# Moving two key copies a batch to ScalarE, constant products in TensorE's waits, and the last output tile in two halves

## The chip, the cores and the metric

The kernel runs on one core of one Trainium2 chip. The core has five engines with a queue of instructions each: TensorE (PE; its weight loads are listed as PEld), VectorE (DVE), ScalarE (ACT), GpSimd (POOL) and SyncE (SP); 16 DMA engines move data. TensorE reads its operands from SBUF and writes to PSUM, which VectorE and ScalarE read. The metric is the time of the program on the device in microseconds (us); smaller is better. The profile is one execution, taken by the hardware profiler.

## What is computed

Two layers follow each other: chunked attention with a few memory keys, and a mixture of experts with noisy top-2 routing over its output.

```python
# attention: q, k, v are (4 batches, 8 heads, 768, 64); mem_k, mem_v (4, 8, 8, 64)
for c in range(nc):                       # 24 chunks of 32 queries
    l_start, r_end = max(0, c_start - 16), min(S, c_end + 8)
    k_full = np.concatenate([mem_k, k[:, :, l_start:r_end]], axis=2)
    v_full = np.concatenate([mem_v, v[:, :, l_start:r_end]], axis=2)
    scores = scale * np.matmul(q_c, k_full.transpose(0, 1, 3, 2))
    a = softmax(scores)
    out[:, :, c_start:c_end] = np.matmul(a, v_full)
# experts: x is (3072, 512), 8 experts, w1 (8, 512, 1024), w2 (8, 1024, 512)
noisy_logits = x @ w_gate + np.log1p(np.exp(x @ w_noise)) * noise
top2 = the two largest of each token; top2_w = softmax over the two
for e in range(8):
    for k in range(2):
        mask = top2[:, k] == e
        out[mask] += top2_w[mask, k, None] * (np.maximum(x[mask] @ w1[e], 0) @ w2[e])
```

## The kernel before

**Attention.** The four batches have three steps each, 12 in all (`NT`; step `i` is batch `i // 3`, position `tp = i % 3`); a step handles two tiles of 128 queries for all eight heads, taken as four pairs. TensorE, ScalarE, VectorE and SyncE follow an order written out by hand in the loop from L568; each engine works through its queue in that order.

A step runs: `scores(i + 1)` for the next step (L408; first eight small products with the memory keys, then, for tile j = 0 and 1 and each of the four pairs, four products with the keys; VectorE then takes the maximum `mx` and subtracts it into `sc`); `turn_p` (L439: TensorE transposes the probabilities, ScalarE copies them to `pT`); `turn_x` for the step before (L472: the same for the step's output `x`, copied to `xT` by ScalarE); `values` (L448: sums and products with the values into `ps_o`, which VectorE divides into the rows of x at L466); `exps` (L434, ScalarE); `gate` for the step before (L481: the router's logits).

**The turn of a batch.** Queries and keys arrive in natural order and have to be turned: `turn` (L393) takes one unit, a pair's queries or keys, through 12 transposes on TensorE into one of three PSUM banks used in rotation. `turns` (L552) copies the result to `qT` or `kT`. A unit of queries is one copy; a unit of keys is two copies of 64 partitions. `KS` (L562) says which engine copies each of the four key units: 1 is ScalarE, 0 VectorE; before, units 0 and 2 are ScalarE's and 1 and 3 VectorE's, so each has four copies a batch. `PLAN` puts the keys at the end of the batch's middle step, so the next step's `scores(i + 1)`, the first of the new batch, waits for them pair by pair. There is one `kT`. On VectorE's queue the copies are followed by a small operation of the router (`facts`, L313, batches 2 and 3), the filling of masked scores, and `mx`.

GpSimd issues the loads (L123 for q, k and v; L78 and L81 for the experts' weights), copies the values of a later batch into another order (`spread_v`, L374), and does part of the router's work (L305 to L348).

**Routing.** Tokens are sorted into 28 lists, one for each pair of experts. A `Route` object does this for a group of rows: `choose` (VectorE, top two), `ranks` (TensorE, L292 on, into `p_rank`), `place` and `slots` (VectorE, one-hot `oh_l`), `weights` and `values` (GpSimd or VectorE, `vals`), `lists` (TensorE, L358, `p_list`). The last two groups, `rb` and `rc`, are handled after the last step (L630 to L660). From the lists come `src`, `dst` and the weights (`decode`).

**Experts.** GpSimd gathers the tokens of each list by indirect DMA from `xd`, the rows of x in DRAM (L677); the first lists are turned by TensorE (`transposes`, L691, into `xTt`), later ones by DMA (L702). 18 steps of one expert and two to four lists follow: `mm1` (L711: 128-column weight tiles, `p_h`, then relu to `h`) and, a step later, `mm2` (L729: eight products of 512 columns into `p_y`; the first expert's result is scaled by ScalarE, the second's added by VectorE at L738). `put` (L682) writes a finished tile by indirect DMA from GpSimd's queue. The tiles of the last two steps are held back and written at the very end, one after the other. `p_y` has two buffers.

PSUM pools of the attention: `psT` (three banks in rotation), `psS` (`ps_s`), `psO` (`ps_o`, one buffer), `psG`.

Of the kernel before, what the change touches and what calls it, by code (L numbers as in the profile page):

```python
# [11 lines left out]
F32 = mybir.dt.float32  # L12
# [3 lines left out]
Alu = mybir.AluOpType  # L16
Act = mybir.ActivationFunctionType
# [5 lines left out]
def kernel(  # L23
# [14 lines left out]
    nc = tc.nc  # L38
    B, H, S, D = q.shape
# [365 lines left out]

    small = psG.tile([128, 4, 128], F32, name="small")

    def scores(t):  # L408
        b, tp = divmod(t, TP)
        ps_s = psS.tile([128, 2, HP, 2, KW], F32, name="ps_s")  # L410
        for j in range(2):
            for pair in range(HP):
                tk = (2 * tp + j) * 128
                nc.tensor.matmul(out=ps_s[:, j, pair, :, 0:NM], lhsT=qT[b % 2][:, pair, tk:tk + 128],
                                 rhs=mkT[:, pair, :, b * NM:(b + 1) * NM], start=True, stop=True)
        for j in range(2):
            for pair in range(HP):
                tk = (2 * tp + j) * 128
                for r in range(4):
                    tr = tk + r * CH  # L420
                    nc.tensor.matmul(out=ps_s[r * CH:(r + 1) * CH, j, pair, :, NM:KW], lhsT=qT[b % 2][:, pair, tr:tr + CH],  # L421
                                     rhs=kT[:, pair, :, tr:tr + WIN], start=True, stop=True, tile_position=(0, r * CH))
# [6 lines left out]
        nc.vector.tensor_reduce(out=mx, in_=s3, axis=AX, op=Alu.max)  # L429
# [15 lines left out]
        nc.scalar.copy(pT, p_p)  # L445
        return pT

    def values(t, pT, between=None):  # L448
        b, tp = divmod(t, TP)
        ps_g = small[:, t % 2, 0:2 * H].rearrange("p (j h) -> p j h", j=2)  # L450
        for x in range(2 * HP):
            j, pair = divmod(x, HP)
            nc.tensor.matmul(out=ps_g[:, j, 2 * pair:2 * pair + 2], lhsT=pT[:, x, :], rhs=ones2,
                             start=True, stop=True)
        ps_o = psO.tile([128, 2, HP, 2, D], F32, name="ps_o")
        for j in range(2):
            for pair in range(HP):
                for r in range(4):
# [63 lines left out]
    with tc.manual_schedule(engines={ET.PE, ET.Activation, ET.DVE, ET.SP}):  # L522
# [28 lines left out]
        nc.vector.tensor_copy(nz.rearrange("p g e -> p e g"), p_nz)  # L551
        def turns(b, units):  # L552
            for u, eng in units:
                for o_, i_ in turn(b, u):
                    (nc.scalar.copy if eng else nc.vector.tensor_copy)(o_, i_)  # L555

        def fill(i, at):
            b, tp = divmod(i, TP)
            if b + 1 < B:
                turns(b + 1, PLAN[min(b, 1)].get((tp, at), ()))  # L560

        KS = ((0, 1), (1, 0), (2, 1), (3, 0))  # L562
        QS = ((4, 1), (5, 1), (6, 1), (7, 1))
        PLAN = ({(1, 2): QS + KS},
                {(1, 1): QS[0:2], (1, 2): QS[2:4] + KS})
# [2 lines left out]
        for i in range(NT):  # L568
# [19 lines left out]
            if i == TP + 2:  # L588
                r0.weights(nc.gpsimd)
                r0.order()  # L590
                r0.values(nc.gpsimd, 0, NV)
            if not last:
                sc = scores(i + 1)

            pTs[i] = turn_p(pbs.pop(i))
            if last:
# [3 lines left out]
            if i:  # L600
                xTs_[i - 1] = turn_x(xrs.pop(i - 1))
            fill(i, 1)
            xrs[i] = values(i, pTs.pop(i), (lambda: gate(i - 1, xTs_.pop(i - 1))) if last else None)
            if last:
                break
            pbs[i + 1] = exps(sc)
# [22 lines left out]

        i = NT - 1  # L630
        keep_x(b, SO - 2, SO, nc.sync)
        xT = turn_x(xrs.pop(i))
        advance(chosen)
        rb.weights(nc.gpsimd)
        rb.values(nc.gpsimd, 0, 2)
        gate(i, xT)
        rc.noise()
        rb.ranks()
# [87 lines left out]
        return h  # L726


    def mm2(h, j, n, w, weight, y=None, home=None):  # L729
        p = psY.tile([128, Dm], F32, name="p_y")  # L730
        for f in range(FB):
            nc.tensor.matmul(out=p, lhsT=h[:, (f * n + j) * 128:(f * n + j + 1) * 128], rhs=w(KP * F + f * Dm, Dm),  # L732
                             start=(f == 0), stop=(f == FB - 1))
        if y is None:
            y = yp.tile([128, Dm], F32, name="y") if home is None else home
            nc.scalar.activation(out=y, in_=p, func=Act.Copy, scale=weight)  # L736
        else:
            nc.vector.scalar_tensor_tensor(out=y, in0=p, scalar=weight, in1=y, op0=Alu.mult, op1=Alu.add)  # L738
        return y


# [176 lines left out]
    def second(job, home=None, held=None):  # L918
# [12 lines left out]
    for i, (b, e, s0, ds_, n, ps_) in enumerate(steps):  # L931
# [54 lines left out]
        if i == 17:  # L986
# [58 lines left out]
```

## Time and profile before

| | |
|---|---|
| median of 3 runs | 349.49 us (349.2 to 350.31) |
| the profiled execution, time | 347.16 us |
| its span, first to last instruction | 345.6 us |
| mean granted TensorE clock | 0.876 |
| TensorE busy | 277.9 us (80%) |
| VectorE busy | 169.7 us (49%) |
| ScalarE busy | 136.0 us (39%) |
| GpSimd busy | 135.4 us (39%) |

How to read the lines that follow. The page cuts the span into 40 equal slices and gives each engine's busy share in tenths, one digit a slice (9 is 90% or more). A line of the timeline is: start and duration in us, engine, line of the kernel, operation, output <- inputs, shape, count; the bracket at its end is the engine's idle time just before it and what ended that. A line of the waits is: who waited for whom, total us, times, longest. Windows give, for a stretch of the span, its length, an engine's busy time and count, the granted TensorE clock (1.00 is full, 0.50 half), the DMA engines' busy share and GB/s.

### The profile page before, as it was taken

The numbers are of one execution on the slowest core, as the hardware profiler recorded it, in microseconds if no ns is written. First come the engines' busy times: TensorE is split into PE (matmuls) and PEld (weight loads), VectorE is DVE, ScalarE is ACT, GpSimd is POOL, SyncE is SP. The second block draws the span as 40 slices with busy tenths as digits, with TensorE's granted clock in tenths as the row PEclk, the third lists the DMA queues.
The fourth block names the chain that finished last, engine by engine and source line by source line (L and its number), as shares of the span: only waits on it lengthen the run. The fifth ranks groups of instructions, "written<-read, shape, count | busy, mean of one in ns | idle before, by whom it ended". The sixth has DMA issues, their size and how long they took to land.

```text
span 345.6 us, 7087 instructions
## 1 busy us (share of the span) xinstructions
PE 277.9 (80%) x2955; PEld 179.2 (52%) x2975; DVE 169.7 (49%) x353; ACT 136.0 (39%) x189; POOL 135.4 (39%) x186
## 2 busy tenths in 40 slices
PE   0357469766756724999998999999999999999991
PEld 0346458655636623855543465764446666555540
DVE  7658367899689886511233202954410233322221
ACT  8823655754745610244321343213244222244310
POOL 6460583466450046822831555352481033201132
PEclk9965855766858865899999999999999999999997
DMA  8999999999999941799999999991289996100012
GB/s 118 227 206 190 248 206 261 228 216 277 239 212 231 235 132 45 131 218 202 167 196 189 255 186 248 169 177 55 74 160 102 171 210 184 57 16 2 26 48 83
DMA packets 49818, 56.97 MB, mean 165 GB/s; under 512 B 16883, under 2 KB 39475, under 8 KB 49780
## 3 DMA queue, kind: packets, MB, share of 16 engines
q0 software_dynamic: 34192, 46.82, 73.4%
q1 hardware_dynamic: 13920, 6.62, 10.0%
q10 hardware_dynamic: 1668, 3.02, 2.6%
q8 instruction: 25, 0.41, 0.5%
q14 instruction: 13, 0.11, 0.1%
HBM read 70.39 MB, written 13.76 MB: 244 GB/s over the span
## 4 chain that ended last, share of the span: by engine, by line
PE 21%; issue 20%; DMA 13%; POOL 5%; DVE 3%; SPq 3%; POOLq 1%; ACT 1%; DVEq 0%; ACTq 0%
PE p_h L720 11%; PE p_y L732 8%; DMA xt<-xd,main_src 6%; DMA xTt<-xt 6%; POOL out_dram L683 4%; SPq L702 3%; DMA out_dram<-y,main_dst 1%; DVE w_all L466 1%; POOL xt L677 0%; PE p_xt L697 0%; POOLq L1040 0%; POOL w_all L861 0%; POOL w_all L862 0%; ACT xT L478 0%; ACT pT L445 0%
## 5 line engine op out<-in xcount | busy, mean ns | idle before, releaser
L720 PE MATMUL p_h<-xTt,w_all 128*128 128x256 bf16 (+3 forms) x669 | 101.5, 310 | 2.0 <-DMA xTt<-xt 1.3
L732 PE MATMUL p_y<-w_all,h 128*128 128x512 bf16 x431 | 98.6, 379 | 0.9
L720 PEld LDWEIGHTS <-w_all 128*128 128x128 bf16 x672 | 65.1, 99 | 36.8 <-issue 2.5
L708 ACT ACTIVATE h<-p_h 128x512 bf16<-128x512 f32 (+1 forms) x79 | 43.5, 550 | 89.6 <-PE p_h L720 85.4
L732 PEld LDWEIGHTS <-h 128*128 128x128 bf16 x448 | 43.7, 98 | 50.2 <-issue 0.2
L706 DVE TENSOR_SCALAR h<-p_h 128x512 bf16<-128x512 f32 (+1 forms) x47 | 29.6, 630 | 75.3 <-PE p_h L720 68.6
L683 POOL DMA_INDIRECT out_dram<-y,main_dst x28 | 30.9, 1105 | 82.9 <-DVE y L738 66.4
L738 DVE SCALAR_TENSOR_TENSOR y<-p_y,main_w,y 128x512 f32<-128x512 f32 x28 | 21.0, 750 | 38.8 <-PE p_y L732 37.3
L677 POOL DMA_INDIRECT xt<-xd,main_src x28 | 28.0, 1000 | 29.9 <-DMA xTt<-xt 18.0
L399 PE MATMUL p_t<-identb,w_all 128*64 128x128 bf16 x384 | 19.2, 269 | 22.8 <-DMA w_all<-in_k_dram 11.6
L736 ACT ACTIVATE y<-p_y,main_w 128x512 f32<-128x512 f32 x28 | 19.2, 687 | 36.5 <-PE p_y L732 35.5
L399 PEld LDWEIGHTS <-w_all 128*64 128x64 bf16 x384 | 16.2, 141 | 25.3 <-DMA w_all<-in_k_dram 12.6
L445 ACT COPY pT<-p_p 128x1024 bf16<-128x1024 bf16 x12 | 12.1, 1010 | 24.7 <-PE p_p L442 24.7
L389 POOL DMA_DIRECT2D w_all<-vd x16 | 11.8, 747 | 19.3 <-DMA vd<-vp 13.6
L466 DVE TENSOR_TENSOR w_all<-ps_o,rs 128x512 bf16<-128x512 f32 x24 | 15.6, 686 | 4.4 <-PE ps_o L459 3.9
L436 ACT ACTIVATE pb<-sc 128x1024 bf16<-128x1024 f32 x12 | 12.8, 1064 | 11.3 <-DVE sc L431 11.3
L421 PE MATMUL ps_s<-kT,qT 128*32 128x112 bf16 x384 | 11.9, 286 | 5.5 <-DVE kT L555 4.7
L374 POOL COPY vp<-w_all 128x1536 bf16<-128x1536 bf16 x8 | 11.5, 1470 | 11.9 <-DMA w_all<-in_v_dram 11.9
L555 DVE COPY kT<-p_t 64x768 bf16<-64x768 bf16 x12 | 11.5, 955 | 7.6 <-PE p_t L399 7.4
L431 DVE TENSOR_TENSOR sc<-ps_s,mx 128x1024 f32<-128x1024 f32 x12 | 14.7, 1225 | 0.8
L429 DVE TENSOR_REDUCE mx<-ps_s 128x16 f32<-128x1024 f32 x12 | 14.7, 1224 | 0.8 <-PE ps_s L421 0.5
L478 ACT COPY xT<-p_x 128x1024 bf16<-128x1024 bf16 x12 | 12.2, 1016 | 2.1 <-PE p_x L476 2.1
(185 smaller groups left out, 283.7 us busy)
## 6 DMA issues: line engine op xcount, KB each, us to landing
w_all<-in_moe_w_dram POOLq DMA_DIRECT2D x16, 1024.0 KB, 18.8
w_all<-in_moe_w_dram POOLq DMA_DIRECT2D x8, 512.0 KB, 12.8
w_all<-in_v_dram POOLq DMA_DIRECT2D x4, 768.0 KB, 11.0
w_all<-in_k_dram POOLq DMA_DIRECT2D x4, 768.0 KB, 19.2
w_all<-in_q_dram POOLq DMA_DIRECT2D x4, 768.0 KB, 16.7
vd<-vp SPq DMA_DIRECT2D x4, 768.0 KB, 7.1
w_all<-vd POOLq DMA_DIRECT2D x8, 384.0 KB, 10.1
w_all<-vd POOLq DMA_DIRECT2D x8, 288.0 KB, 10.9
```

Of the source, the lines that this page charges most:

```text
L399: nc.tensor.transpose(out=p_t[own(par), s, :], in_=src[:, 2 * pair + par, s * D:(s + 1) * D], identity=identb, tile_position=(0, par * 64))
L429: nc.vector.tensor_reduce(out=mx, in_=s3, axis=AX, op=Alu.max)
L431: nc.vector.tensor_tensor(out=sc, in0=s3, in1=bc(mx, KW), op=Alu.subtract)
L466: nc.vector.tensor_tensor(out=xr[:, j, 0:Dm].rearrange("p (h d) -> p h d", h=H), in0=ps_o[:, j].rearrange("p c a d -> p (c a) d"), in1=bc( ...
L677: i = nc.gpsimd.indirect_dma_start(out=xts[key].bitcast(I32), out_offset=None, in_=xd, in_offset=bass.IndirectOffsetOnAxis(ap=ix, axis=0))
L683: i = nc.gpsimd.indirect_dma_start(out=out.rearrange("n (r c) -> (n r) c", r=cuts), out_offset=bass.IndirectOffsetOnAxis(ap=ix, axis=0), i ...
L706: nc.vector.tensor_scalar(out=out_, in0=in_, scalar1=0.0, scalar2=None, op0=Alu.max)
L708: nc.scalar.activation(out=out_, in_=in_, func=Act.Relu)
L720: nc.tensor.matmul(out=o, lhsT=w(kp * F + f * 128, 128), rhs=x[:, kp], start=(kp == 0), stop=(kp == KP - 1))
L732: nc.tensor.matmul(out=p, lhsT=h[:, (f * n + j) * 128:(f * n + j + 1) * 128], rhs=w(KP * F + f * Dm, Dm), start=(f == 0), stop=(f == FB - 1))
L736: nc.scalar.activation(out=y, in_=p, func=Act.Copy, scale=weight)
L738: nc.vector.scalar_tensor_tensor(out=y, in0=p, scalar=weight, in1=y, op0=Alu.mult, op1=Alu.add)
```

## The change

Three things are changed.

1. `KS` gives key units 0, 2 and 3 to ScalarE and only unit 1 to VectorE, in batches 1 to 3: six copies for ScalarE and two for VectorE in each. (The new comparison `eng > part` would also allow a unit to be split; the values used, 0 and 2, do not split any, and a query unit has one part.)
2. `warm(p, n)` issues n products of the constant matrix `ones` with the identity repeated four times, 128 x 128 by 128 x 512, into a PSUM buffer that is free at that time and whose contents are overwritten or never read. They stand: in the first scores of batches 1 to 3, four before pair 1 and one before pair 3 of tile 0; two before the values of steps 10 and 11; and after the last step two before `gate`, eight before `rc.ranks`, five before the second part of the lists and four after it.
3. The last tile of the last step is computed in two halves of 256 columns, each with eight products and an addition of its own; its write waits for both.

```diff
-    def scores(t):
+    def scores(t, waits=None):
...
             for pair in range(HP):
+                if waits is not None and j == 0:
+                    waits(pair)
...
+    def warm(p, n):
+        for _ in range(n):
+            nc.tensor.matmul(out=p, lhsT=ones, rhs=identb.unsqueeze(1).to_broadcast([128, 4, 128]), start=True, stop=True)
+
-    def values(t, pT, between=None):
+    def values(t, pT, between=None, fillers=0, home=None):
         b, tp = divmod(t, TP)
+        ps_o = psO.tile([128, 2, HP, 2, D], F32, name="ps_o") if home is None else home
+        if fillers:
+            warm(ps_o[:, 0].rearrange("p c a d -> p (c a d)"), fillers)
...
-                for o_, i_ in turn(b, u):
-                    (nc.scalar.copy if eng else nc.vector.tensor_copy)(o_, i_)
+                for part, (o_, i_) in enumerate(turn(b, u)):
+                    (nc.scalar.copy if eng > part else nc.vector.tensor_copy)(o_, i_)
...
-        KS = ((0, 1), (1, 0), (2, 1), (3, 0))
+        KS = ((0, 2), (1, 0), (2, 2), (3, 2))
...
+            home, waits = None, None
+            if tp == TP - 1 and more:
+                home = psO.tile([128, 2, HP, 2, D], F32, name="ps_o")
+                waits = lambda pair: warm(home[:, 0].rearrange("p c a d -> p (c a d)"), (0, 4, 0, 1)[pair])
             if not last:
-                sc = scores(i + 1)
+                sc = scores(i + 1, waits)
...
-            xrs[i] = values(i, pTs.pop(i), (lambda: gate(i - 1, xTs_.pop(i - 1))) if last else None)
+            xrs[i] = values(i, pTs.pop(i), (lambda: gate(i - 1, xTs_.pop(i - 1))) if last else None,
+                            2 if i > 3 * TP else 0, home)
...
+        p_w = psS.tile([128, 2, HP, 2, KW], F32, name="ps_s")[:, 0].rearrange("p c a w -> p (c a w)")
...
+        warm(p_w, 2)
         gate(i, xT)
...
         rc.weights(nc.gpsimd, 2, 3)
+        warm(p_w, 8)
         rc.ranks()
...
         rc.lists(0, 2, head=rb)
+        warm(p_w, 5)
...
         rc.lists(2, NV, head=rb)
+        warm(p_w, 4)
...
-    def mm2(h, j, n, w, weight, y=None, home=None):
-        p = psY.tile([128, Dm], F32, name="p_y")
-        for f in range(FB):
-            nc.tensor.matmul(out=p, lhsT=h[:, (f * n + j) * 128:(f * n + j + 1) * 128], rhs=w(KP * F + f * Dm, Dm),
-                             start=(f == 0), stop=(f == FB - 1))
+    def mm2(h, j, n, w, weight, y=None, home=None, cuts=1):
+        c = Dm // cuts
+        ps = [psY.tile([128, c], F32, name="p_y") for _ in range(cuts)]
+        for x, p in enumerate(ps):
+            for f in range(FB):
+                nc.tensor.matmul(out=p, lhsT=h[:, (f * n + j) * 128:(f * n + j + 1) * 128],
+                                 rhs=w(KP * F + f * Dm + x * c, c), start=(f == 0), stop=(f == FB - 1))
...
+            for x, p in enumerate(ps):
+                o = y[:, x * c:(x + 1) * c]
+                nc.vector.scalar_tensor_tensor(out=o, in0=p, scalar=weight, in1=o, op0=Alu.mult, op1=Alu.add)
...
-            y = mm2(h, j, n, w, wt, None if first else ys.pop(k), home)
+            y = mm2(h, j, n, w, wt, None if first else ys.pop(k), home,
+                    2 if end and j == len(tiles) - 1 else 1)
...
-    second(prev, held=held)
+    second(prev, held=held, end=True)
```

The built program differs from the one before in one more place: on VectorE the first `xTt` copy stands two operations of `main_w` later.

More of the change, by code (lines that the diff above doesn't have):

```diff
@@ L454, in values @@
                              start=True, stop=True)
-        ps_o = psO.tile([128, 2, HP, 2, D], F32, name="ps_o")
         for j in range(2):
@@ L726, in mm1 @@
         return h
-    def mm2(h, j, n, w, weight, y=None, home=None):
-        p = psY.tile([128, Dm], F32, name="p_y")
-        for f in range(FB):
-            nc.tensor.matmul(out=p, lhsT=h[:, (f * n + j) * 128:(f * n + j + 1) * 128], rhs=w(KP * F + f * Dm, Dm),
-                             start=(f == 0), stop=(f == FB - 1))
+    def mm2(h, j, n, w, weight, y=None, home=None, cuts=1):
[5 more added lines that the diff above has]
+                                 rhs=w(KP * F + f * Dm + x * c, c), start=(f == 0), stop=(f == FB - 1))
         if y is None:
             y = yp.tile([128, Dm], F32, name="y") if home is None else home
-            nc.scalar.activation(out=y, in_=p, func=Act.Copy, scale=weight)
+            nc.scalar.activation(out=y, in_=ps[0], func=Act.Copy, scale=weight)
         else:
-            nc.vector.scalar_tensor_tensor(out=y, in0=p, scalar=weight, in1=y, op0=Alu.mult, op1=Alu.add)
+            for x, p in enumerate(ps):
+                o = y[:, x * c:(x + 1) * c]
+                nc.vector.scalar_tensor_tensor(out=o, in0=p, scalar=weight, in1=o, op0=Alu.mult, op1=Alu.add)
         return y
@@ L916, in few2, with second @@
         return y
-    def second(job, home=None, held=None):
+    def second(job, home=None, held=None, end=False):
         h, n, w, tiles = job
         for j, (k, wt, ix, first) in enumerate(tiles):
-            y = mm2(h, j, n, w, wt, None if first else ys.pop(k), home)
+            y = mm2(h, j, n, w, wt, None if first else ys.pop(k), home,
+                    2 if end and j == len(tiles) - 1 else 1)
             if first:
```

## The prediction

> **What bounds the kernel now.** I read the page's slices first, then TensorE's waits, then the timeline around the turns from one batch to the next.
>
> ```profile
> span 345.6 us, 7087 instructions
> ...
> PE   0357469766756724999998999999999999999991
> ...
> DVE  7658367899689886511233202954410233322221
> ```
>
> From the 17th slice on (about 138 us) TensorE is full: the mixture of experts is bound by it. Before that no engine is full for long and the time is set by chains of waits, which end in the first gather of tokens (`xt<-xd`). Whatever moves that gather moves all behind it.
>
> The three turns differ. At batch 2's, the two engines copy side by side (the columns: start, duration, engine, line, what; in brackets the idle time before and what ended it):
>
> ```profile
> 63.71 0.86 PE L399 MATMUL p_t<-identb,w_all 128*64 128x128 bf16 x24 [2.33 <-DMA w_all<-in_q_dram]
> ...
> 68.44 3.22 ACT L555 COPY kT<-p_t 64x768 bf16<-64x768 bf16 x4
> 68.83 3.88 DVE L555 COPY kT<-p_t 64x768 bf16<-64x768 bf16 x4 [0.29 <-PE p_t L399]
> ...
> 70.84 0.28 PE L421 MATMUL ps_s<-kT,qT 128*32 128x112 bf16 x8
> ...
> 72.10 0.90 POOL L123 DMA_DIRECT2D w_all<-in_k_dram  x1 [3.39 <-DMA w_all<-in_v_dram]
> 72.74 3.17 DVE L313 TENSOR_TENSOR facts<-ii 128x6 bf16<-128x6 f32 x1
> 72.77 0.66 PE L421 MATMUL ps_s<-kT,qT 128*32 128x112 bf16 x20 [0.79 <-DVE kT L555]
> ...
> 72.99 2.88 POOL L374 COPY vp<-w_all 128x1536 bf16<-128x1536 bf16 x2
> ...
> 75.79 1.05 PE L459 MATMUL ps_o<-w_all,pT 128*32 128x128 bf16 x32
> ...
> 76.19 1.23 DVE L429 TENSOR_REDUCE mx<-ps_s 128x16 f32<-128x1024 f32 x1
> ...
> 78.95 1.29 DVE L466 TENSOR_TENSOR w_all<-ps_o,rs 128x512 bf16<-128x512 f32 x2
> ```
>
> The scores end at 72.77 + 0.66 = 73.43, yet `mx`, which reads them, starts at 76.19. Between them stands the six-column `facts` operation, 3.17 us long, ending (75.91) as GpSimd's copies do (75.87).
>
> Batch 3's turn:
>
> ```profile
> 92.18 0.42 PEld L399 LDWEIGHTS <-w_all 128*64 128x64 bf16 x13 [0.29 <-DMA w_all<-in_k_dram]
> ...
> 94.53 3.22 ACT L555 COPY kT<-p_t 64x768 bf16<-64x768 bf16 x4
> ...
> 96.18 0.85 PE L399 MATMUL p_t<-identb,w_all 128*64 128x128 bf16 x12 [0.96 <-ACT kT L555]
> ...
> 96.98 3.87 DVE L555 COPY kT<-p_t 64x768 bf16<-64x768 bf16 x4
> ...
> 97.27 0.28 PE L421 MATMUL ps_s<-kT,qT 128*32 128x112 bf16 x4
> ...
> 100.88 0.19 DVE L313 TENSOR_TENSOR facts<-ii 128x8 bf16<-128x8 f32 x1
> 100.91 0.66 PE L421 MATMUL ps_s<-kT,qT 128*32 128x112 bf16 x20 [1.58 <-DVE kT L555]
> ...
> 101.87 1.23 DVE L429 TENSOR_REDUCE mx<-ps_s 128x16 f32<-128x1024 f32 x1
> ```
>
> Here VectorE comes to its four copies 2.45 us after ScalarE, so pair 3 (its last two) is what the scores wait for, until 100.85. The same `facts` operation takes 0.19 us here.
>
> **The change part by part.** *Copies.* Pair 3's two copies move to ScalarE: 3.22/4 = 0.805 us each there, 0.97 on VectorE.
> Batch 2: ScalarE's six end at 68.44 + 6 x 0.805 = 73.27, which is 0.56 later than VectorE's end (72.71); the scores end at 73.27 + 0.66 = 73.93 and `mx` could start 0.30 behind (as from 101.57 to 101.87), at 74.23. VectorE is done with its two copies at 68.83 + 1.94 = 70.77 and comes to `facts` 2.2 us before GpSimd's copies, so I count 0.19 for it. `mx` gains 76.19 - 74.23 = 1.96. The division L466 also needs the values, which now come 0.5 later (76.84 + 0.5 = 77.34), so it starts at about 77.4 instead of 78.95: **1.55 us**.
> The Trainium skill ("SBUF — State Buffer", Who interferes with whom) says that a tensor_tensor with two SBUF inputs and a GpSimd operation reading SBUF exclude each other for a whole instruction, the first to issue going first. By it the early `facts` is free, as I count it. Were the 3.17 us a wait for something else on GpSimd, the term would be 0: that is rival B.
> Can batch 3 use 1.55 us? Its keys land at 92.18: their load is issued at 72.10, when an earlier load has landed, and no copy moves that; with 12 transposes (0.85 at most) the first copy can start at 93.05, 1.48 before 94.53; with faster transposes a little sooner. I take 1.5.
> Batch 3: from ScalarE's first copy to the scores' end is now 100.91 + 0.66 - 94.53 = 7.04; then 6 x 0.805 + 0.66 + 0.1 of handover = 5.59. Pair 3's transposes wait for pair 0's copies (96.18) and are done 1.65 + 0.85 = 2.5 after the first copy, before ScalarE wants them at 3.2. Gain **1.45 us**.
> Batch 1's copies end some 0.4 later in the same way; that and more lies under the 2.33 us in which TensorE waits for `in_q` at 63.71, a landing that no copy moves. Counted 0; without that cover it would cost 0.4.
>
> *Fillers in the scores.* Four before pair 1, one before pair 3. The price of one comes from the chain of waits:
>
> ```profile
> 196.71 6.91 PE p_y L732 x32
> 203.62 3.49 PE p_h L720 x32
> ```
>
> 32 products of 512 columns take 6.91 us, 0.216 each at full clock; at half clock I take twice that, 0.43. Five are 1.1 to 2.2 us. At batch 2 pair 0 is done by 71.12 and pair 3's keys come at 73.27: 2.15 us of room, so they fit. At batch 3, pair 0 ends at about 97.55 - 1.5 = 96.05, and pair 3's keys come at 94.53 - 1.5 + 4.83 = 97.86: 1.81 of room, of which two pairs' products take 0.3; at half clock the fillers overrun by 0.65, at full clock not at all. I charge **-0.3 us**. Behind them in TensorE's queue stand the remaining scores, and VectorE's `mx` behind these. The first filler also waits until VectorE has read the buffer of the values' sums; that read stands ahead of the key copies on VectorE and is over by then. On ScalarE the copy `pT` stands behind pair 3, but its transposes follow the scores anyway.
>
> *Fillers before the values of the last batch's second and third pair of tiles, and in the routing's tail* (2, 2, then 2, 8, 5, 4):
>
> ```profile
> PE p_rank L294 <- DVE ohp L288: 3.9, 1, 3.9
> ...
> PE p_list L358 <- DVE vals L348: 2.3, 1, 2.3
> ...
> PE p_xt L697 <- DMA xt<-xd,main_src: 1.7, 1, 1.7
> ```
> ```profile
> 105.03 1.29 DVE L466 TENSOR_TENSOR w_all<-ps_o,rs 128x512 bf16<-128x512 f32 x2 [0.52 <-PE ps_o L459]
> ...
> 115.75 0.37 PE L453 MATMUL small<-ones,pT 128*128 128x2 bf16 x8 [0.31 <-ACT pT L445]
> ```
>
> Eight at half clock are 3.4 against 3.9 of wait, five 2.15 against 2.3, four 1.7 against 1.7: all covered, and a lost cover costs 0.43 a filler. (In the third of these waits the build also moves the first `xTt` copy behind two small `main_w` operations, which VectorE does while the gather is awaited: 0.) Two before the values at 115.75 have 0.31 of room: 0.55 lost at half clock, 0.1 at full. Against this a fuller clock shortens the values, for which VectorE waited 0.52 at 105.03. Between -0.55 and +0.7 I take **+0.2 us**.
>
> *The clock itself.* Windows of 3.41 us, cut where the granted clock changes (TensorE's busy time and count, its clock, DMA share, GB/s):
>
> ```profile
> 105.93:109.35 3.42, 2.76 (x102) 1.00 1.16 212
> 109.35:112.76 3.41, 1.39 (x48) 1.00 1.13 280
> ...
> 136.65:140.06 3.41, 2.90 (x29) 0.50 0.33 99
> 140.06:143.48 3.42, 3.42 (x40) 1.00 0.47 98
> ```
>
> The first stretch of the experts runs at half clock for 2.90 us of work, worth up to 1.45. It is counted 0, for the work ahead of this wait is hidden under it:
>
> ```profile
> 189.64 7.07 PE L720 MATMUL p_h<-xTt,w_all 128*128 128x512 bf16 x31 [1.31 <-DMA xTt<-xt]
> ```
>
> That landing hangs on the queue of gathers, transposes and weights behind the first gather; a quicker start only makes the 1.31 us longer.
> The Trainium skill ("TensorE: Matmul & The Clock Gate", Part 1) has the clock fall only after an idle window, and holds it to be binary. By it the fillers would keep the clock full to the end (rival C). The row from 109.35, 1.39 us of work and half clock behind it at 112.76, speaks against so lenient a rule.
>
> *Last tile in halves.*
>
> ```profile
> 336.67 0.75 DVE L738 SCALAR_TENSOR_TENSOR y<-p_y,main_w,y 128x512 f32<-128x512 f32 x1 [1.03 <-PE p_y L732]
> 338.34 0.75 DVE L738 SCALAR_TENSOR_TENSOR y<-p_y,main_w,y 128x512 f32<-128x512 f32 x1 [0.92 <-PE p_y L732]
> ...
> 338.55 0.98 POOL L683 DMA_INDIRECT out_dram<-y,main_dst  x1 [1.66 <-issue]
> 339.83 0.98 POOL L683 DMA_INDIRECT out_dram<-y,main_dst  x1 [0.30 <-issue]
> ```
>
> 16 products of 256 columns at 3.49/32 = 0.109 are 1.74 us, as 8 of 512 (1.73): nothing on TensorE. VectorE's last operation halves to 0.4-0.5 and ends 0.25 to 0.35 sooner. But the last write follows the one before it (338.55 + 0.98 + 0.30), and that one starts just after 338.33, 0.9 after its own tile was ready and when VectorE comes to its last operation. If it hangs on that, it starts near 337.7, and the last write is bound by its own tile at about 339.2: 0.65 gained; if not, 0 (or 0.1 lost, as the second half takes over a buffer that VectorE frees at 337.42). I take **0.4 us**.
>
> Sum: 1.5 + 1.45 - 0.3 + 0.2 + 0.4 = 3.25 us. The profiled execution took 347.16 us (span 345.6), so 343.9 by its own time; the median of the runs shown is 349.49, 0.7% above it, and the sum off the median gives **346.2 us**.
>
> **The rivals.**
> B. The `facts` operation is not freed (it waits for GpSimd, or in most executions it misses the copies by a hair: it started 0.25 us before them). Then batch 2's term is 0, and 3.25 - 1.5 = 1.75: 347.7 us. For it: one row alone shows the stall. Against: its end falls on that of GpSimd's copies within 0.04.
> C. The clock stays full from batch 2 on. Then the -0.3 goes, the values give their 0.7 instead of 0.2, batch 2's division waits no more for the values (+0.25), the lists' products shorten (+0.3), and the end gives its 0.65: 4.85, so 344.6 us. Against it stands the row from 109.35.
> D. Slower: a filler costs more than it is given room for. Place: in front of the scores, values, ranks and lists; price: its overrun. With c for one at half clock, 29c less the rooms 2.15 + 1.5 + 0.31 + 3.9 + 2.3 + 1.7 = 11.9 is lost. From c = 0.53 this eats the gain without the filler terms (3.35); at 0.60 (0.43, and a load of its own weights that nothing hides) it is 5.5 and the result 349.49 - 3.35 + 5.5 = 351.6 us. For it: no row shows such a product at half clock. Against: the 0.216 of the row at 196.71 holds the loads too.
> E. The gain stops at the gather, which needs the rows of x written:
>
> ```profile
> 122.15 0.32 SPq L491 DMA_DIRECT2D xd<-w_all  x1
> ...
> 132.62 1.61 POOL L677 DMA_INDIRECT xt<-xd,main_src  x1 [2.23 <-DVE facts L313]
> ```
>
> If that write, issued in the middle of the weights' loads, lands only when they end, a gather some 3 us sooner would wait for it, and only the end's 0.4 is left: 349.1 us. Against: 10.5 us lie between them.
>
> **How the numbers follow.** Forecast 0.46, B 0.2, C 0.14, D 0.1, E 0.1. A measurement of this kernel can tell about 0.3% (1.05 us) from no change, so faster means below 348.44: forecast, B and C, 0.80; the same: E, 0.10; slower: D, 0.10. The range leaves out D, E and the far end of C. Below it ends at 343.8: C, and about half of the 1.45 us at the experts' start not hidden after all. Above it ends at 348.8: B without the end's 0.4, and the fillers before the values costing 0.55 instead of bringing 0.2.
>
> **What would show it.** Right: the `facts` operation behind two copies at 0.2 us; `mx` of batch 2 about 0.3 behind the scores; the first copy of batch 3 near 93; the first gather near 129.7; the wait at 189 grown. Wrong: the 3.17 us again; TensorE ending a filler after pair 3's keys are there, or a p_rank, p_list or p_xt that waits for nothing but fillers; a gather that waits for `xd`; the last write but one still near TensorE's end.

## The result, and the profile after

| | before | after |
|---|---|---|
| median | 350.12 us (349.2 to 352.85, 6 runs) | 345.73 us (344.92 to 346.93, 6 runs) |
| the profiled execution, time | 347.16 us | 345.12 us |
| its span | 345.6 us | 343.5 us |
| mean granted TensorE clock | 0.876 | 0.921 |
| VectorE / ScalarE busy | 169.7 / 136.0 us | 161.0 / 141.0 us |

Both medians are from the same chip; the ratio is 0.9863, with a 95% interval of 0.9825 to 0.9901, a gain of 4.4 us by the medians where 3.25 were forecast, and 345.73 us where 346.2 (343.8 to 348.8) was. Ratios, here and below, compare the faster runs alone, so they are not quotients of the medians, and e12's trace is of one of its kernel's longer runs, so only what lies ahead of its first gather is used. The two profiled executions differ by 2.0 us only, and the section after the experiments says why.

The slices of the page, as they were shown of before:

```profile
span 343.5 us, 7180 instructions
...
PE   0356484777786868799999999999999999999993
...
DVE  7658426769769787411224201964410134313232
```

The end is as full as it was. What changed lies ahead of it. Batch 2's turn on the timeline (columns as in the prediction; lines behind L415 have moved by two to twenty-two, so L563 is the key copy and L431 the maximum):

```profile
70.94 4.84 ACT L563 COPY kT<-p_t 64x768 bf16<-64x768 bf16 x6
71.28 1.92 DVE L563 COPY kT<-p_t 64x768 bf16<-64x768 bf16 x2 [0.18 <-PE p_t L399]
...
73.24 0.18 DVE L313 TENSOR_TENSOR facts<-ii 128x6 bf16<-128x6 f32 x1
...
73.50 1.04 PE L452 MATMUL ps_o<-identb,ones 128*128 128x512 bf16 x4
...
75.33 2.88 POOL L374 COPY vp<-w_all 128x1536 bf16<-128x1536 bf16 x2
...
75.83 0.43 PE L423 MATMUL ps_s<-kT,qT 128*32 128x112 bf16 x20 [0.76 <-ACT kT L563]
...
76.56 1.23 DVE L431 TENSOR_REDUCE mx<-ps_s 128x16 f32<-128x1024 f32 x1
...
79.31 1.29 DVE L474 TENSOR_TENSOR w_all<-ps_o,rs 128x512 bf16<-128x512 f32 x2
...
81.73 0.28 PE L423 MATMUL ps_s<-kT,qT 128*32 128x112 bf16 x4 [1.62 <-issue]
```

The `facts` operation is over 1.9 us before GpSimd's copies begin, and takes 0.18 us instead of 3.17. The scores still end with the keys, not with the products put in front of them: TensorE waits 0.76 us for pair 3. `mx` follows the scores' end (75.83 + 0.43) by 0.30. From ScalarE's first key copy to `mx` it is 5.62 us, where it was 76.19 - 68.44 = 7.75. The last row is a hole in TensorE's queue of 1.62 us, in which it waits for nothing that the profile shows.

Batch 3's turn:

```profile
94.38 1.90 PE L399 MATMUL p_t<-identb,w_all 128*64 128x128 bf16 x36 [2.12 <-DMA w_all<-in_k_dram]
...
95.04 4.84 ACT L563 COPY kT<-p_t 64x768 bf16<-64x768 bf16 x6 [0.19 <-PE p_t L399]
...
97.15 1.92 DVE L563 COPY kT<-p_t 64x768 bf16<-64x768 bf16 x2
...
98.00 1.89 PE L452 MATMUL ps_o<-identb,ones 128*128 128x512 bf16 x4
...
99.10 0.20 DVE L313 TENSOR_TENSOR facts<-ii 128x8 bf16<-128x8 f32 x1
...
100.12 0.61 PE L452 MATMUL ps_o<-identb,ones 128*128 128x512 bf16 x1
...
100.66 0.66 PE L423 MATMUL ps_s<-kT,qT 128*32 128x112 bf16 x20
...
101.63 1.23 DVE L431 TENSOR_REDUCE mx<-ps_s 128x16 f32<-128x1024 f32 x1
```

TensorE now waits 2.12 us for the keys, since the turn ahead of it is shorter (and the keys landed 2.2 us later than in before's execution). Behind that the products overrun: ScalarE's copies end at 99.88, the twenty last scores start at 100.66, without a wait. Four products took 1.89 us here and 1.04 at batch 2; the clock was half here and full there. First copy to `mx`: 6.59 us, before 7.34.

The route's tail and the first gather:

```profile
124.00 2.56 PE L452 MATMUL ps_s<-identb,ones 128*128 128x512 bf16 x8
128.01 0.22 PE L294 MATMUL p_rank<-ohp,tri 128*128 128x112 bf16 x1 [1.45 <-DVE ohp L288]
...
130.25 2.32 PE L452 MATMUL ps_s<-identb,ones 128*128 128x512 bf16 x5
132.76 1.11 PE L358 MATMUL p_list<-vals,oh_l 128*128 128x112 bf16 x10 [0.19 <-DVE vals L348]
133.67 1.91 PE L452 MATMUL ps_s<-identb,ones 128*128 128x512 bf16 x4
135.62 0.38 PE L715 MATMUL p_xt<-identb,xt 128*128 128x128 bf16 x4
...
136.52 1.05 PE L738 MATMUL p_h<-xTt,w_all 128*128 128x128 bf16 x16 [0.51 <-DVE xTt L716]
...
139.57 0.40 PE L715 MATMUL p_xt<-identb,xt 128*128 128x128 bf16 x4 [1.78 <-DMA xt<-xd,main_src]
```

```profile
132.06 1.61 POOL L695 DMA_INDIRECT xt<-xd,main_src  x1 [2.23 <-DVE facts L313]
```

The ranks and the lists still wait for VectorE behind the products, for 1.45 and 0.19 us: covered. Behind the last four the turn of the first gathered tokens (`p_xt`, 135.62) waits for nothing: they use up the room. It starts 3.56 us after the gather, where it started 3.48 after it before (132.62 to 136.10). The experts' first 16 products take 1.05 us at full clock; right behind them TensorE waits 1.78 us for the next gather.

The last writes, and VectorE's additions for the last tiles:

```profile
335.05 0.98 POOL L701 DMA_INDIRECT out_dram<-y,main_dst  x1 [0.70 <-DVE y L760]
337.69 0.98 POOL L701 DMA_INDIRECT out_dram<-y,main_dst  x1 [1.66 <-DVE y L760]
338.97 0.97 POOL L701 DMA_INDIRECT out_dram<-y,main_dst  x1 [0.30 <-issue]
```

```profile
335.80 1.30 DVE L760 SCALAR_TENSOR_TENSOR y<-p_y,main_w,y 128x512 f32<-128x512 f32 x2 [1.03 <-PE p_y L752]
337.68 0.48 DVE L760 SCALAR_TENSOR_TENSOR y<-p_y,main_w,y 128x256 f32<-128x256 f32 x1 [0.57 <-PE p_y L752]
```

All three writes stand 0.86 us earlier than before (335.91, 338.55 and 339.83). The distances between them, 2.64 and 1.28 us, are the same. The bracket of the write at 337.69 names VectorE, but the operation on that write's own tile was over at 336.55 (the first of the two at 335.80, 0.75 us long).

### The profile page after: what moved, and what is told of

Its sections match the earlier page's. It is cut to its first block, busy times and chain, and to the rows that moved or that the text cites. A ratio compares the mean times of both kernels' runs of the same rounds, so it can differ in the third digit from the quotient of the medians.

```text
span 343.5 us, 7180 instructions
## 1 busy us (share of the span) xinstructions
PE 284.4 (83%) x3001; PEld 177.0 (52%) x3021; DVE 161.0 (47%) x348; ACT 141.0 (41%) x195; POOL 135.0 (39%) x186
## 4 chain that ended last, share of the span: by engine, by line
PE 46%; DMA 11%; DVE 3%; SPq 3%; POOL 2%; issue 1%; ACT 0%; POOLq 0%; DVEq 0%
PE p_y L752 22%; PE p_h L738 21%; DMA xt<-xd,main_src 6%; DMA xTt<-xt 5%; SPq L720 3%; POOL xt L695 1%; DVE w_all L474 1%; PE p_x L484 0%; POOLq L1063 0%; ACT xT L486 0%; PE p_y L930 0%; PE p_h L910 0%; PE p_p L444 0%; POOL w_all L81 0%; PE p_list L358 0%
## 5 line engine op out<-in xcount | busy, mean ns | idle before, releaser
L752 PE MATMUL p_y<-w_all,h 128*128 128x512 bf16 (+1 forms) x439 | 98.8, 375 | 0.9
L738 PEld LDWEIGHTS <-w_all 128*128 128x128 bf16 x672 | 64.0, 98 | 36.0 <-issue 1.6
L752 PEld LDWEIGHTS <-h 128*128 128x128 bf16 x456 | 44.4, 98 | 49.9 <-issue 0.4
L760 DVE SCALAR_TENSOR_TENSOR y<-p_y,main_w,y 128x512 f32<-128x512 f32 (+1 forms) x29 | 21.2, 732 | 38.4 <-PE p_y L752 36.9
L563 ACT COPY kT<-p_t 64x768 bf16<-64x768 bf16 x18 | 14.3, 793 | 3.7 <-PE p_t L399 3.5
L431 DVE TENSOR_REDUCE mx<-ps_s 128x16 f32<-128x1024 f32 x12 | 14.7, 1222 | 0.8 <-PE ps_s L423 0.5
L423 PE MATMUL ps_s<-kT,qT 128*32 128x112 bf16 x384 | 10.8, 260 | 2.4 <-issue 1.6
```

Source lines behind the costliest of these rows:

```text
L738: nc.tensor.matmul(out=o, lhsT=w(kp * F + f * 128, 128), rhs=x[:, kp], start=(kp == 0), stop=(kp == KP - 1))
L760: nc.vector.scalar_tensor_tensor(out=o, in0=p, scalar=weight, in1=o, op0=Alu.mult, op1=Alu.add)
```

## The experiments

Each kernel was timed beside the kernel before on one chip. The stretches in the last four columns come from one timeline each: from ScalarE's first key copy to the start of `mx` in batch 2 and in batch 3; from batch 2's first key copy to the first gather; from the start of the last output write to the span's end.

| kernel | median us | ratio (95%) | batch 2 | batch 3 | to gather | last write to end |
|---|---|---|---|---|---|---|
| before | | | 7.75 | 7.34 | 64.18 | 5.77 |
| after | 345.73 | 0.9863 (0.9825 to 0.9901) | 5.62 | 6.59 | 61.12 | 4.53 |
| e1_copies | 349.11 | 0.9897 (0.9856 to 0.9938) | 5.85 | 5.86 | 61.28 | 5.28 |
| e2_fillers | 350.05 | 0.9955 (0.9933 to 0.9977) | 7.04 | 7.38 | 65.02 | 4.82 |
| e3_halves | 350.29 | 0.9965 (0.9941 to 0.9989) | 7.81 | 7.31 | 64.68 | 4.40 |
| e4_facts | 349.64 | 0.9951 (0.9916 to 0.9985) | 5.38 | 7.32 | 63.24 | 5.14 |
| e5_no_score | 347.89 | 0.9867 (0.9822 to 0.9912) | 5.86 | 5.85 | 60.99 | 4.78 |
| e6_no_tail | 348.04 | 0.9899 (0.9847 to 0.9951) | 5.63 | 5.66 | 61.50 | 4.73 |
| e7_whole | 348.86 | 0.9898 (0.9846 to 0.9950) | 5.63 | 6.59 | 62.01 | 5.17 |
| e8_both | 348.87 | 0.9900 (0.9866 to 0.9935) | 5.63 | 5.85 | 61.75 | 5.07 |
| e9_branch | 345.45 | 0.9872 (0.9807 to 0.9938) | 5.63 | 5.67 | 60.98 | 4.37 |
| e10_no_products | 345.95 | 0.9854 (0.9815 to 0.9892) | 5.63 | 5.86 | 61.96 | 4.22 |
| e11_both | 346.39 | 0.9886 (0.9826 to 0.9946) | 5.63 | 5.86 | 62.14 | 4.41 |
| e12_third | 348.65 | 0.9963 (0.9923 to 1.0004) | 7.16 | 5.85 | 63.21 | |

The ratios of one group (e1 to e4, e5 to e8, e9 to e12) share the runs of before, whose medians were 351.41, 352.66 and 350.37 us: an error in these moves all four of a group together. Medians of different groups are not compared.

**e1_copies**, the key copies alone.

```diff
-        KS = ((0, 1), (1, 0), (2, 1), (3, 0))
+        KS = ((0, 1), (1, 0), (2, 1), (3, 1))
```

> Only the key copies move (six on ScalarE, two on VectorE in batches 1 to 3). If the copies carry the change (the prediction's terms 1.5 + 1.45, and no filler to overrun): 3 us faster, the facts operation of batch 2 at 0.2 us, the way from the first copy of batch 3 to the end of its scores 5.6 us instead of 7.04. If the clock carries it: at most 1.5 us faster, since the batch's scores end only when ScalarE is done.

```profile
70.59 4.84 ACT L555 COPY kT<-p_t 64x768 bf16<-64x768 bf16 x6
71.04 1.92 DVE L555 COPY kT<-p_t 64x768 bf16<-64x768 bf16 x2
...
72.99 0.18 DVE L313 TENSOR_TENSOR facts<-ii 128x6 bf16<-128x6 f32 x1
...
74.48 2.88 POOL L374 COPY vp<-w_all 128x1536 bf16<-128x1536 bf16 x2
...
76.44 1.23 DVE L429 TENSOR_REDUCE mx<-ps_s 128x16 f32<-128x1024 f32 x1
```

1.0% or 3.6 us: the copies alone are most of the change. Both stretches shrink, by 1.90 and 1.48 us, and the stretch to the gather by 2.9.

**e2_fillers**, all constant products alone: the change with the key copies as before and the last tile whole.

```diff
-        KS = ((0, 2), (1, 0), (2, 2), (3, 2))
+        KS = ((0, 2), (1, 0), (2, 2), (3, 0))
...
-    second(prev, held=held, end=True)
+    second(prev, held=held)
```

> Only the constant products, key copies as before and the last tile whole. By the prediction's terms about 0 (-0.3 + 0.2), the facts operation stays at 3 us. If the clock carries the change: 2 us or more faster, with the clock full in more windows between 100 and 137 us. If a filler costs more than its room: slower.

0.45% by the times, but the timeline shows nothing of it: batch 3 takes 7.38 us as before, and to the gather it is 65.02 us. The 0.7 us at batch 2 are a `facts` operation that met GpSimd's copies a little later and waited 2.31 us instead of 3.17. e10 takes the question up.

**e3_halves**, the last tile in halves alone: the change with the key copies as before and no products.

```diff
-        for _ in range(n):
+        for _ in range(0):
...
-        KS = ((0, 2), (1, 0), (2, 2), (3, 2))
+        KS = ((0, 2), (1, 0), (2, 2), (3, 0))
```

> Only the last tile in halves. By the prediction 0.4 us faster (0 to 0.65). If the last write but one hangs on the write before it and not on VectorE (2.64 us from start to start in both profiles), no difference, and the same 2.64 us again.

0.35%, the interval just clear of no change. The distances of the last writes are 2.64 and 1.28 us here too. What differs is what follows the last write: 4.40 us, 5.77 before.

**e4_facts**, before with `r0.order()`, which holds the `facts` operation, ahead of batch 2's key copies.

```diff
             if i == TP + 2:
                 r0.weights(nc.gpsimd)
-                r0.order()
                 r0.values(nc.gpsimd, 0, NV)
...
             if i == TP + 1:
                 advance(chosen)
+                r0.order()
```

> The kernel before, with the facts operation of batch 2's turn put ahead of the four key copies on VectorE instead of behind them; nothing else. If the 3.17 us are a stall against GpSimd's copies and gate what follows: the operation takes 0.2 us, mx starts 0.3 behind the scores, 1.5 us or more faster. If the operation waits for something on GpSimd: it stays long and holds the key copies, slower. If batch 3's keys land too late to use it: no difference.

```profile
69.68 0.17 DVE L313 TENSOR_TENSOR facts<-ii 128x6 bf16<-128x6 f32 x1
...
70.34 3.88 DVE L555 COPY kT<-p_t 64x768 bf16<-64x768 bf16 x4 [0.49 <-PE p_t L399]
...
74.28 2.88 POOL L374 COPY vp<-w_all 128x1536 bf16<-128x1536 bf16 x2
...
75.23 1.23 DVE L429 TENSOR_REDUCE mx<-ps_s 128x16 f32<-128x1024 f32 x1
```

With the copies still four to four, batch 2's stretch falls to 5.38 us, lower than with any copies moved. So its gain is the stalled operation, not ScalarE's share. Batch 3 stays at 7.32, and 1.7 us are won.

**e5_no_score**, the change without the products in the scores.

```diff
-                sc = scores(i + 1, waits)
+                sc = scores(i + 1)
```

> The change without the 15 constant products in the waits of the batches' first scores (its other products, the key copies and the halves stay). Theory 1, from the traces of the changed kernel and of the copies alone: at batch 3 the products run at half clock and the scores' end comes 6.28 us after ScalarE's first key copy, where without them the wait for the last copies is the end; here that stretch should be about 5.5 us (the copies alone: 95.38 to the memset's end near 101.2, 5.9 to the reduction), so 0.7 us are won there; batch 2 loses up to 0.6 us if the clock is no longer full. Net between -0.7 and +0.6 us against the changed kernel, ratio to before about 0.985 to 0.988. Rival 2, the products pay as a whole (the products alone measured 0.9955): without them the kernel loses 1 us or more against the changed one, ratio about 0.990.

Batch 3 takes 5.85 us (5.5 was expected) where the change took 6.59: its products cost 0.74 us there. At batch 2 the change is 0.24 shorter (5.62 against 5.86). That difference is the last twenty scores, 0.43 us at full clock and 0.66 at half, and the products are not shown to be its cause: e8, e10 and e11 have none there and take 5.63. The ratio is that of the change: theory 1.

**e6_no_tail**, the change without the products before the values and in the tail.

```diff
-                            2 if i > 3 * TP else 0, home)
+                            0, home)
...
-        warm(p_w, 2)
...
-        warm(p_w, 8)
...
-        warm(p_w, 5)
...
-        warm(p_w, 4)
```

> The change without the 2 products before each turn's values from the 14th turn on and without the 19 in the route's last section. Theory 1: between the last scores and the first gather TensorE is not what is waited for (the reduction of batch 3 to the first gather took 30.75 us before, 30.43 after, 30.63 with the copies alone, 32.02 with the products alone), so nothing changes: ratio about 0.986 as with the change, and the experts' first products run at half clock (about 1.9 us for 16) while the following wait for the gathered tokens shrinks by as much. Rival 2: the products are worth the 1.6 us that the products alone measured, mostly here, and the ratio goes to about 0.991.

```profile
94.62 4.85 ACT L563 COPY kT<-p_t 64x768 bf16<-64x768 bf16 x6
...
97.18 1.04 PE L452 MATMUL ps_o<-identb,ones 128*128 128x512 bf16 x4
...
99.55 0.43 PE L423 MATMUL ps_s<-kT,qT 128*32 128x112 bf16 x20
...
100.28 1.23 DVE L431 TENSOR_REDUCE mx<-ps_s 128x16 f32<-128x1024 f32 x1
```

The ratio can't tell the theories apart. The trace shows the same product at full clock in batch 3: four take 1.04 us, fit in front of the keys, and the stretch is 5.66, 0.2 better than in any trace without products. So there they go with 0.2 us gained or 0.7 lost, depending on the clock. From batch 3's `mx` to the gather it is 31.02 us, 30.43 with the tail's products, 30.75 before. The experts' first 16 products take 1.87 us, as expected, and no wait follows them.

**e7_whole**, the change with the last tile whole.

```diff
-    second(prev, held=held, end=True)
+    second(prev, held=held)
```

> The change with the last output tile whole again. Theory 1: the last two writes are issued 2.64 and 3.92 us behind the third from the end in every trace so far, with halves or without, so the halves gain nothing at the issue, and the ratio stays at about 0.986. Rival 2, the halves are worth the 1.2 us that they measured alone, by what follows the last issue (3.4 to 3.6 us to the span's end with halves, 3.8 to 4.8 without): the ratio goes to about 0.990 and the last issue stands 4.2 us or more before the span's end.

The last write follows at the same distance, and 5.17 us lie behind its start. Both this and the ratio of 0.990 are what rival 2 expected, but the interval takes in theory 1's 0.986 too.

**e8_both**, before with both edits, that of e1 (written as `KS = ((0, 2), (1, 0), (2, 2), (3, 2))`) and that of e4.

> Before, with the change's two key copies a batch on ScalarE and with the operation that writes facts put ahead of VectorE's key copies in batch 2. Theory 1: both edits free the same operation, batch 2's gain is one and the same 1.5 to 2 us, and batch 3's 1.5 us comes with the copies: about 3.6 us in all as with the copies alone, ratio about 0.990. Rival 2, the two add up (1.0 % and 0.5 %): ratio about 0.985, since VectorE's reduction would start right behind the scores in both batches and the operation is out of the way.

0.9900, as the copies alone, not 0.985: the two edits win the same time in batch 2. Theory 1.

**e9_branch**, the change with one more output write behind GpSimd's conditional branch, to see what the 2.64 us are.

```diff
-            second(prev, held=held if i == len(steps) - 1 else None)
+            second(prev, held=held if i >= len(steps) - 2 else None)
```

> The change, with one more output write put behind the program's conditional branch on GpSimd's queue (six instead of five; the writes and their order are the same). In all ten traces the last but one write starts 2.64 us behind the one before it, with a hole of 1.44 us in which GpSimd waits for nothing that the profile shows, and the last follows 1.28 us later; VectorE's rows for its tile end 0.9 us before the hole does. Theory 1, the hole belongs to a place in GpSimd's program (the fourth write behind the branch), not to the data: it goes in front of the write before, so the gap of 2.64 us shrinks to 1.3 to 1.8 us and the last write starts 0.3 to 0.5 us earlier against TensorE's last output product (1.33 us behind it in the changed kernel). Rival 2, the hole hangs on the tile or on the queue of writes: the gaps stay at 2.64 and 1.28 us. The time itself moves by 0.5 us at most, ratio about 0.986.

```profile
333.82 0.98 POOL L701 DMA_INDIRECT out_dram<-y,main_dst  x1 [0.69 <-DVE y L760]
336.45 0.98 POOL L701 DMA_INDIRECT out_dram<-y,main_dst  x1 [1.65 <-DVE y L760]
337.73 0.98 POOL L701 DMA_INDIRECT out_dram<-y,main_dst  x1 [0.30 <-issue]
```

A miss: 2.63 and 1.28 us again. Theory 1 falls.

**e10_no_products**, the change without any product (the edits of e5 and e6 in one).

> The change without any constant product: key copies and halves alone. Theory 1, the products are worth nothing together (what they win at full clock they lose at half clock, and the gather doesn't wait for TensorE): from batch 2's first key copy to the first gather 61.0 to 61.8 us as in the traces with the copies (61.1, 61.3, 61.0, 61.5, 62.0, 61.8; 64.2 to 65.0 without the copies), ratio 0.985 to 0.988. Rival 2, they are worth the 0.45 % that they measured alone: ratio 0.990 or more.

0.9854, at or below the change's 0.9863, and 61.96 us to the gather: theory 1. The 38 products (15 in the scores, 4 before the values, 19 after the last step) are worth nothing that can be measured beside the copies, though intervals of 0.4% to either side leave room for a microsecond or more. They did raise the granted clock: it was 0.92 to 0.94 in the change's runs, and in e9's on the same chip, and 0.87 to 0.90 here.

**e11_both**, e10 with eight writes behind the branch.

```diff
-            second(prev, held=held if i == len(steps) - 1 else None)
+            second(prev, held=held if i >= len(steps) - 4 else None)
```

> Key copies and halves without products, and eight output writes behind the branch instead of five. Theory 1 (the hole belongs to a place in GpSimd's program): the hole leaves the last two writes, the last but one follows the write before by about 1.8 us (as the tile's row ends), and the last one starts 0.5 us earlier against TensorE's end; 0.3 to 0.6 us faster than the kernel without products, ratio about 0.984. Rival 2: gaps of 2.64 and 1.28 us as before, no gain.

The distances are 2.61 and 1.29 us, the ratio is no better: the hole stays with the write, wherever the branch stands.

**e12_third**, before with the copies six to two in batch 3 alone.

```diff
...
+        K3 = ((0, 2), (1, 0), (2, 2), (3, 2))
...
-                {(1, 1): QS[0:2], (1, 2): QS[2:4] + KS})
+                {(1, 1): QS[0:2], (1, 2): QS[2:4] + KS},
+                {(1, 1): QS[0:2], (1, 2): QS[2:4] + K3})
```

> Before, with the key copies six to two in batch 3 alone. Theory 1, batch 3's gain is carried whole: ScalarE's first key copy to the maximum's reduction 7.3 to 5.9 us in batch 3, 7.75 with the stalled facts operation (about 3 us) in batch 2, and from batch 2's first key copy to the first gather 64.6 to about 63.1 us; 1.5 us faster, ratio about 0.9955. Rival 2, the gather waits for something that the scores don't move: the stretch stays at 64.2 to 65.0 us, ratio 1.

```profile
74.34 2.88 POOL L374 COPY vp<-w_all 128x1536 bf16<-128x1536 bf16 x2
...
74.83 2.42 DVE L313 TENSOR_TENSOR facts<-ii 128x6 bf16<-128x6 f32 x1
...
96.04 4.84 ACT L555 COPY kT<-p_t 64x768 bf16<-64x768 bf16 x6
...
101.89 1.22 DVE L429 TENSOR_REDUCE mx<-ps_s 128x16 f32<-128x1024 f32 x1
```

Batch 2 stalls again (until 77.25, GpSimd's copies until 77.22), batch 3 takes 5.85 us, and to the gather it is 63.21. 0.9963 is the forecast, though the interval just reaches 1.

## Why the prediction was right, point by point

**Where the time went.** The sum's place was right. From batch 2's first key copy to the first gather the kernels with the old copies (before, e2, e3) took 64.63 us in the mean, e4, which frees batch 2 alone, 63.24, e12, which frees batch 3 alone, 63.21, and the nine with the new copies 61.53 (60.98 to 62.14). That is 1.39 us for batch 2, 1.42 for batch 3 and 3.10 for both. The first two rest on one trace each, and the traces of a group lie up to 0.84 us (old copies) and 1.16 us (new) apart, so they are good to about half a microsecond.

**Batch 2: 1.5 forecast, 1.4 measured.** The freed `facts` operation was the cause, as forecast, by e4 and e8. Rival B is out: behind two copies the operation took 0.18 us, and it was over before GpSimd's copies began. Where it stalled (3.17, 2.31, 3.16 and 2.42 us in before, e2, e3 and e12), it ended within 0.05 us of GpSimd's copies. "SBUF — State Buffer" in the Trainium skill (Who interferes with whom) agrees that these exclude each other. The row of before leaves its rule that the first to issue goes first open: the operation's row starts at 72.74, GpSimd's at 72.99, and yet VectorE's ends last. The carrying was capped as argued: the stretch itself shrinks by 1.9 to 2.4, and then TensorE waits for `in_k`, 2.12 us after the change where before it waited 0.29. Ahead of that cap the term was too small: the division came 8.37 us behind the first key copy (70.94 to 79.31), before 10.51, so 2.14 sooner and not 1.55. The prediction let it wait for values that come 0.5 later; they ended 7.89 us behind the first key copy (78.83), before 8.40 (76.84), since their 32 products took 0.63 us at full clock and 1.05 before.

**Batch 3: 1.45 forecast, 1.42 to 1.49 measured** (e12; 7.34 against 5.85 in e5).

**Products in the scores: -0.3 forecast; 0.74 lost at half clock, 0.2 better at full.** The mechanism (they fit at full clock, overrun at half) was right and the two prices nearly: 1.89/4 = 0.47 at half clock for 0.43, 1.04/4 = 0.26 at full for 0.216. Halfway between the two cases lies the forecast, but the 0.2 is not shown to be the products' doing (e5); e5 and e10 show no net effect.

**Products before the values and in the tail: +0.2 forecast, 0 shown.** From batch 3's `mx` to the gather the five kernels with the tail's products (after, e2, e5, e7, e9) took 30.4 to 32.0 us, the nine without them 30.6 to 31.7. Rival D is out: the kernel is not slower, and the products that a wait did not cover cost little. Those before step 10's values made the sums behind them start 1.62 us after `p_x` (113.64 to 115.26), before 1.36 (114.39 to 115.75). The sign that `p_xt` would wait for nothing but products came, for 0.08 us. E is out too: the gather waits 2.23 us for a `facts` operation of VectorE, as before, not for the rows of x, and it came 3.1 us sooner behind batch 2's first key copy. e2's own 0.45% has no row to stand on; e10 speaks against it, and an error in the runs of before that e1 to e4 share could make part of it. This stays open.

**The experts' start: 0 forecast, 0 found, by another wait.** The first 16 products took 1.05 us instead of 1.86, but then TensorE waited 1.78 us for the second gather. So it came to the wait at 189 hardly sooner (188.25 against 188.33), and that wait did not grow, as I had said it would, but shrank:

```profile
188.78 3.40 PE L738 MATMUL p_h<-xTt,w_all 128*128 128x512 bf16 x15 [0.53 <-DMA xTt<-xt]
```

In these two traces the landing keeps its distance from the first gather, as the prediction had it: 56.58 us (132.06 to 188.64), 56.89 before (132.62 to 189.51). But from the gather to the row that waited for the landing it is 56.7 and 57.0 us in these two and 57.0 to 59.7 in e3, e9, e10, e11 and e12, so it hangs on more than the gather.

**The halves: +0.4 forecast, in the wrong place.** This is the step that failed: the last write but one does not hang on VectorE's last operation. That operation now starts elsewhere and in two parts, and the write keeps its 2.64 us. Nor did VectorE end 0.25 to 0.35 us sooner: counted from the start of the third write from the end, it ended after 3.11 us (335.05 to 338.16), before 3.18 (335.91 to 339.09). TensorE, where the prediction counted nothing or 0.1 us, ended its last product 0.2 us later in halves, after 2.59 us (337.64) and not 2.39 (338.30). The gain is behind the last write instead. The seven kernels with halves need 4.22 to 4.78 us from there to the end (mean 4.49), the six with a whole tile 4.82 to 5.77 (mean 5.21): 0.7 us, though the nearest two, e5 and e2, are only 0.04 apart. That the term came out positive is luck. It is not the transfers: in windows of 0.2 us the DMA engines move their last bytes 2.8 to 3.6 us behind the last write's start, with halves and without. No row says what is shorter there, nor what the 1.66 us of idle GpSimd ahead of the last write but one are; e9 and e11 exclude a place in GpSimd's program counted from the branch.

**The sum.** 3.1 us ahead of the gather (which holds the products) and 0.7 at the end make 3.8, inside the 3.5 to 6.1 us of the measured ratio on 350.12. The forecast had 2.85 and 0.4 in these places, so its 3.25 fell short by 0.25 and 0.3 there and by what the interval leaves open. The profiled executions show only 2.0 us because before's was ahead when it came to batch 2: its first key copy there is at 68.44, in all others at 69.56 to 71.20 (70.94 after; `in_q` landed 2.5 us later). For the same reason the signs "first copy of batch 3 near 93" and "gather near 129.7" did not come (95.04 and 132.06); counted from the landing of `in_k` the gather came 37.68 us behind, before 40.44. Behind the gather single executions tell still less: to the last write they took from 206.91 us (after; before 207.21) to 211.5, with no order by the parts that they had.

**The clock (rival C)** was not full to the end: 0.921 in the mean. The windows after batch 2's turn:

```profile
74.18:77.60 3.42, 2.31 (x47) 1.00 1.03 213
77.60:81.01 3.41, 2.20 (x78) 1.00 1.19 168
81.01:84.42 3.41, 2.46 (x33) 0.50 1.23 290
```

A window with 2.20 us of work was followed by half clock, so a few products in the gaps do not hold it. By the rule in the Trainium skill ("TensorE: Matmul & The Clock Gate", Part 1) it would have stayed full, as no window was idle; the measurement decides against it.

## What to carry to other kernels

A tiny operation of 0.2 us that takes 3 is waiting for something: see what else ends at its end, and move it ahead of that; e4 won batch 2's time without moving any copy. Work put into a wait must fit at half clock too: here it did not keep the clock full. Where a kernel's later part varies by 4 us between traced executions, judge an edit of 1 to 3 us by the stretch that it touches, from one landmark to the next, and by medians, not by the end of one trace.

## What was not expected of the hardware

A queue can stand still with no wait that the profile shows. TensorE did so in the middle of 32 equal products, for 1.62 us until 81.73. The place is fixed in its queue and not in its data: in all eight traces that show this hole (after, e6 to e12; 0.19 to 2.17 us) exactly 988 products are recorded ahead of it. It stands behind 15 of the 32 where batches 1 and 2 have their ten constant products and behind 25 where they have not. What TensorE waits for there, no row says. GpSimd stood idle for 1.63 to 1.66 us before the last write but one in every trace, with five, six and eight writes behind its branch; before the last write it was idle for 0.30 to 0.32.

And the clock changed on a fixed grid: in before at 34.25, 37.66, 41.08, 61.56, 64.97 and 68.38, all multiples of 3.413 us apart. Which stretch gets the half clock differs from execution to execution: of the four traces with new copies and products in the scores, batch 3's products ran at half clock in after and e7 and at full clock in e6 and e9.
